# Linear attention and FFN on one core: W1 loads regrouped, the order table solved anew, warm-up matmuls of 512 columns

## The chip, the cores and the metric

The kernel runs on one core of a Trainium2 chip. The metric is the device time of one execution in microseconds (us); a kernel is quoted by the median of its fast executions, with the range. The kernel before took 301.82 us (301.79 to 301.85, 3 runs). Every later comparison has its own runs of the kernel before on the same chip, so that only numbers of one table row belong together. Three executions in the whole study took 479, 588 and 743 us, 1.6 to 2.5 times the usual time; they are called the slow executions below, and no comparison uses them.

## The reference, cut to what matters

```python
# q, k, v: (8 batches, 8 heads, 576 tokens, 64)
q_s = softmax(q, over the 64)          # per token
k_s = softmax(k, over the 576 tokens)  # per column
kv  = einsum('bhsd,bhse->bhde', k_s, v)
attn = einsum('bhsd,bhde->bhse', q_s, kv)
x = attn.transpose(0, 2, 1, 3).reshape(4608, 512)
h = x @ w_in                            # 512 x 2048
g = where(h > 0, h, exp(min(h, 0)) - 1) # ELU
return g @ w_out                        # 2048 x 512
```

Nearly all the arithmetic is the two large products: 576 matmuls of 128 x 128 by 512 columns for each of them.

## The kernel before: the parts that the argument touches

The 4608 tokens go through in nine blocks of 512. For a block, the first product runs in eight groups, each of 8 matmuls (two tiles of 128 features by four slices of 128 inputs); VectorE and ScalarE turn each group into a part of `GT` (ELU), and the second product reads `GT` as its stationary side.

Every engine works through a fixed list. The program first describes all operations, numbered as they are described; a table `ORDER` then says in which order each engine issues them. Nothing is decided at run time but the waits.

```python
ORDER = {
    "pe": (
        "30 28 32 45 43 47 50 67 54 68 69 70 77 81 85 92 114 102 89 128 136 127 135 129 137 106 130 "
        "138 108 149 151 125 148 156 133 131 155 150 139 157 152 145 172 174 158 171 173 232 238 237 "
        # ... (cut; lists for act, dve, gp and sp follow)
```

Group g of the first product, in whole or in two halves (two of the four input slices each):

```python
    def hg_mm(self, j, g, ps, key, half=None):
        # ... (cut)
            for t in range(2):
                tt = 2 * g + t
                for kc in kcs:
                    last = e.matmul(P[:, t * 512:(t + 1) * 512],
                                    self.W1[:, kc, tt * 128:(tt + 1) * 128],
                                    self.XT[:, kc, rc:rc + BLK], start=(kc == 0), stop=(kc == 3))
```

The W1 loads, the first block's order of groups, and the warm-up matmuls, which fill TensorE's idle time at the start:

```python
        for g0, g1, half in ((0, 2, 0), (0, 2, 1), (2, 5, None), (5, 8, None)):
            self.load_w1(g0, g1, half, -30, [gate, self.ident] if half == 0 else ())
        # ... (cut)
        S.spare = lambda count: lambda e: [e.matmul(
            self.PS[0][:, 0:128], self.ID[:, :], self.ID[:, :], start=True, stop=True)
            for _ in range(count)][-1]
        # ... (cut)
        for half in range(2):
            for g in range(2):
                self.hg_mm(0, g, turns[g], key, half)
        for g in range(8):
            self.hg(0, g, turns[g], key, "da"[g % 2], g > 1)
```

The softmax here doesn't subtract the row's maximum and nothing guards it: scores larger than these inputs give would overflow.

## Time and profile before

| quantity | before |
| --- | --- |
| median time | 301.82 us |
| TensorE busy | 285.5 us of a span of 300.2 |
| first product of the first block | 14.78 us |
| wait for W1's third load | 1.28 us, ending at 20.96 |
| TensorE clock at full speed from | 12.80 us |
| other holes of TensorE after 50 us that exceed 0.2 us | one, 0.34 us at 66.68 |

In the code lines of this kernel L403 is a transpose, L456 the product k x v ("kv"), L487 the attention product ("ao"), L543 the first large product, L588 the second, L653 a warm-up matmul; L572, L576 and L578 are VectorE's part of the ELU, L559 and L570 ScalarE's. Of the names, `PS` is the memory for TensorE's results, `XT` the attention result that the first product reads, `qsT` the transposed q and `MBLK` the scaled kv result that the attention product reads, and `ESB` the exponentials of the ELU. In kernels whose table is a few lines longer the same lines are shifted by the same few lines.

A table of stretches (start and end, length, then busy us and number of instructions for PE, PEld, DVE, ACT and POOL; then granted clock, DMA share, GB/s). TensorE's timeline (start, length, engine, line, operation, count).

```profile
52.00:60.00 8.00, 8.00 (x103) 6.43 (x104) 7.08 (x8) 7.70 (x9) 1.30 (x2) 1.00 1.09 317
60.00:68.00 8.00, 7.83 (x58) 5.81 (x45) 7.58 (x14) 7.03 (x8) 0.00 (x0) 1.00 1.02 272
68.00:80.00 12.00, 12.00 (x55) 9.74 (x54) 6.90 (x9) 11.74 (x14) 0.00 (x0) 1.00 0.84 229
```

**A measure used below.** Idle times tell of one hole at a time. To see where a lead is won and lost, I use a "lag": each matmul that the trace records is given the step that it takes unhindered (0.2267 us for a 512-column product, 0.0125 for one kv matmul, 0.14 for an attention product, 0.056 for a transpose, none for warm-up), these are summed in order of time, and the lag is the start time less that sum (its own step included), averaged over the matmuls that start within 1 us of the stated time. A lag that grows means that TensorE waited or ran slowly; two kernels are compared at one time by the difference. All kernels do the same work, so the lag at 290 us orders the profiled runs.

### The profile page before, as it was taken

Reading aid. Unit: us, or ns where it says so; the run is one execution under the profiler, and the core shown is the slowest. Engines: PE = TensorE matmul, PEld = TensorE weight load, DVE = VectorE, ACT = ScalarE, POOL = GpSimd, SP = SyncE. Lnnn points to the kernel's source line nnn. Section 1 sums busy time; section 2 is a strip of 40 time slices with the busy share of each in tenths; the row PEclk is TensorE's granted clock in tenths of the full one; section 3 lists DMA queues with packets and bytes.
Section 4 is the critical chain, followed back from the end, with each engine's and each line's share of the span. In section 5 each row is a group of like instructions: output and inputs, shape, how many; then the busy total and the mean of one; then the engine's idle time right before and its main releaser. Section 6 shows DMA issues by size and latency. Waiting matters only on the chain.

```text
span 300.2 us, 4404 instructions
## 1 busy us (share of the span) xinstructions
PE 285.5 (95%) x1846; PEld 234.1 (78%) x1846; DVE 188.8 (63%) x244; ACT 181.5 (60%) x211; POOL 22.1 (7%) x33
## 2 busy tenths in 40 slices
PE   0789999999999999999999999999999999999995
PEld 0658877878888888888888888888888888888883
DVE  2957954898496768766767783878355436565500
ACT  5847948989868676673966677835441623434211
POOL 0950155100000000000000000000000000000000
PEclk9999999999999999999999999999999999999999
DMA  7999996999367593569931958203221201031224
GB/s 263 387 382 391 389 359 234 309 284 265 105 212 240 126 311 70 188 143 239 295 67 41 261 149 227 59 2 70 59 58 29 61 11 35 0 90 38 49 52 105
DMA packets 35283, 49.96 MB, mean 166 GB/s; under 512 B 16320, under 2 KB 16320, under 8 KB 35264
## 3 DMA queue, kind: packets, MB, share of 16 engines
q1 hardware_dynamic: 29680, 34.09, 41.0%
q0 software_dynamic: 5504, 15.47, 15.9%
q8 instruction: 14, 0.23, 0.3%
q10 hardware_dynamic: 80, 0.13, 0.1%
q14 instruction: 5, 0.04, 0.0%
HBM read 36.70 MB, written 9.44 MB: 154 GB/s over the span
## 4 chain that ended last, share of the span: by engine, by line
PE 88%; DMA 5%; DVE 4%; POOL 1%; ACT 1%; SPq 0%; issue 0%
PE PS L588 43%; PE PS L543 40%; DMA W<-in_moe_w_in_dram 3%; PE PS L487 3%; DMA KR<-in_k_dram 2%; PE PS L456 1%; DVE GT L578 1%; POOL W L332 1%; DVE ESB L576 1%; DVE QS L380 0%; DVE ZQ L372 0%; DVE GT L572 0%; DVE MBLK L469 0%; ACT ESB L559 0%; PE PS L403 0%; SPq L315 0%
## 5 line engine op out<-in xcount | busy, mean ns | idle before, releaser
L543 PE MATMUL PS<-XT,W 128*128 128x512 f32 x576 | 140.8, 391 | 1.9 <-DMA W<-in_moe_w_in_dram 1.3
L588 PE MATMUL PS<-W,GT 128*128 128x512 f32 x576 | 141.2, 391 | 0.0
L543 PEld LDWEIGHTS PS<-XT,W 128*128 128x128 f32 x576 | 106.9, 188 | 25.1 <-DMA W<-in_moe_w_in_dram 1.7
L588 PEld LDWEIGHTS PS<-W,GT 128*128 128x128 f32 x576 | 107.1, 188 | 21.9 <-DVE GT L572 0.3
L559 ACT ACTIVATE ESB<-PS 128x1024 f32<-128x1024 f32 x72 | 73.6, 1027 | 68.9 <-PE PS L543 67.1
L576 DVE TENSOR_SCALAR ESB<-ESB 128x1024 f32<-128x1024 f32 x64 | 44.1, 691 | 73.3 <-ACT ESB L559 72.8
L578 DVE TENSOR_TENSOR GT<-ESB,PS 128x1024 fp32r<-128x1024 f32 x64 | 77.8, 1218 | 1.8
L605 ACT ACTIVATE OSB<-PS 128x512 f32<-128x512 f32 x32 | 18.6, 596 | 23.8 <-PE PS L588 23.8
L509 ACT ACTIVATE XT<-PS 128x512 fp32r<-128x512 f32 (+6 forms) x32 | 19.4, 609 | 16.5 <-PE PS L487 14.7
L372 DVE TENSOR_REDUCE ZQ<-QR 128x18 f32<-128x1152 f32 x16 | 21.5, 1346 | 5.0 <-ACT QR L352 4.9
L380 DVE TENSOR_TENSOR QS<-QR,RZQ 128x1152 f16<-128x1152 f32 x16 | 21.7, 1356 | 0.3
L352 ACT ACTIVATE QR<-QR 128x1152 f32<-128x1152 f32 x16 | 18.6, 1161 | 3.1 <-DMA QR<-in_q_dram 3.1
L356 ACT ACTIVATE KR<-KR 128x1152 bf16<-128x1152 f32 x16 | 18.5, 1160 | 0.5 <-DMA KR<-in_k_dram 0.5
L487 PE MATMUL PS<-qsT,MBLK 128*128 128x320 f32 (+5 forms) x64 | 14.2, 307 | 0.1
L431 ACT ACTIVATE qsT<-QT 128x1152 fp32r<-128x1152 f16 x12 | 14.0, 1166 | 0.3 <-DMA QT<-QS 0.3
L365 ACT ACTIVATE VB<-VR 128x1152 bf16<-128x1152 f32 (+1 forms) x12 | 13.5, 1125 | 0.8 <-DMA VR<-in_v_dram 0.8
L487 PEld LDWEIGHTS PS<-qsT,MBLK 128*128 128x128 f32 x64 | 11.4, 190 | 3.1 <-DVE MBLK L469 1.1
L572 DVE SCALAR_TENSOR_TENSOR GT<-PS,ESB 128x1024 fp32r<-128x1024 f32 x8 | 9.8, 1222 | 3.6 <-ACT ESB L570 3.6
L403 PE MATMUL PS<-ID,QS 128*128 128x128 f16 x36 | 3.2, 244 | 9.1 <-DVE QS L380 9.1
L403 PEld LDWEIGHTS PS<-ID,QS 128*128 128x128 f16 x36 | 2.5, 112 | 9.6 <-DVE QS L380 9.1
L469 DVE TENSOR_TENSOR MBLK<-PS,RZK 64x128 fp32r<-64x128 f32 x32 | 9.1, 283 | 0.8
L570 ACT ACTIVATE ESB<-ESB 128x1024 f32<-128x1024 f32 x8 | 8.4, 1056 | 0.2
(28 smaller groups left out, 58.8 us busy)
## 6 DMA issues: line engine op xcount, KB each, us to landing
out_dram<-OSB SPq DMA_DIRECT2D x63, 128.0 KB, 2.4
QR<-in_q_dram SPq DMA_DIRECT2D x12, 576.0 KB, 4.9
KR<-in_k_dram SPq DMA_DIRECT2D x12, 576.0 KB, 5.8
VR<-in_v_dram SPq DMA_DIRECT2D x12, 576.0 KB, 5.6
W<-in_moe_w_out_dram POOLq DMA_DIRECT2D x4, 1024.0 KB, 19.3
W<-in_moe_w_in_dram POOLq DMA_DIRECT2D x4, 768.0 KB, 10.3
QR<-in_q_dram POOLq DMA_DIRECT2D x4, 576.0 KB, 11.1
KR<-in_k_dram POOLq DMA_DIRECT2D x4, 576.0 KB, 6.0
```

The costliest lines, as they stand in the source:

```text
L352: S.add("act", t_act(1152, False), lambda e: e.activation(flat(q), flat(q), AF.Exp), key - 3, X=[f"qR{i}"], follow=self.table)
L356: S.add("act", t_act(1152, False), lambda e: e.activation(ek[:, :, :, :].rearrange("p h c d -> p (h c d)"), flat(k), AF.Exp), key - 2, X=[ ...
L372: S.add("dve", t_dve(1152), lambda e: e.tensor_reduce(self.ZQ[i][:, :, :].rearrange("p h c -> p (h c)"), q[:, :, :, :].rearrange("p h c d ...
L380: S.add("dve", t_dve(1152), lambda e: e.tensor_tensor(qso, q[:, :, :, :], rz, ALU.mult), key - 3, R=[f"qR{i}", f"RZQ{i}"], W=[f"QS{self.al ...
L487: last = e.matmul(P[:, y:y + n_], M[:, f, :], T[:, c0:c1, f * 64:f * 64 + 64], start=True, stop=True)
L509: S.add("act", t_act((h1 - h0) * n_, True), lambda e, dst=dst, src=src: e.activation(dst, src, AF.Copy), key, W=W, X=X)
L543: last = e.matmul(P[:, t * 512:(t + 1) * 512], self.W1[:, kc, tt * 128:(tt + 1) * 128], self.XT[:, kc, rc:rc + BLK], start=(kc == 0), stop ...
L559: S.add("act", t_act(1024, True), lambda e: e.activation(esb[:, :], P[:, :], AF.Exp), key, W=[f"E{i}"], X=banks)
L576: S.add("dve", t_dve(1024, 2), lambda e: e.tensor_scalar(esb[:, :], esb[:, :], 1.0, -1.0, ALU.min, ALU.add), key, X=[f"E{i}"])
L578: S.add("dve", t_dve(1024), lambda e: e.tensor_tensor(gt, esb[:, :], P[:, :], ALU.max), key, R=[f"E{i}"], W=gw, X=banks)
L588: last = e.matmul(dst, GT[:, jj, ts * 128:(ts + 1) * 128], self.W2[:, jj, :], start=(jj == 0), stop=(jj == 15))
L605: S.add("act", t_act(512, True), lambda e: e.activation(osb[:, :], src, AF.Copy), key, W=[f"O{i}0", f"O{i}1"], X=[f"b{bk}"])
```

## The change

W1's loads are cut so that group 2 comes with groups 0 and 1 in the two half loads, and groups 3-4 and 5-7 follow. The order table is solved anew, with W1's loads shifted. The warm-up matmuls become 512 columns wide, a quarter as many. The intent is to remove the wait for the third load.

```diff
-        "30 28 32 45 43 47 50 67 54 68 69 70 77 81 85 92 114 102 89 128 136 127 135 129 137 106 130 "
-        "138 108 149 151 125 148 156 133 131 155 150 139 157 152 145 172 174 158 171 173 232 238 237 "
+        "30 28 32 43 45 47 50 67 54 68 70 71 69 72 82 86 93 115 103 90 129 128 137 136 131 139 107 "
+        "130 138 109 151 152 150 126 134 149 132 156 157 158 140 173 146 153 159 172 174 175 233 238 "
 ... (the rest of TensorE's list, and the lists of the other four engines, cut)
-                count = int(idle / 80)
-                if count > 1 and all(d.end < free for d in self.spare_after):
-                    p = Op("pe", count * 57, self.spare(count), 0)
+                count = int(idle / 230)
+                if count > 0 and all(d.end < free for d in self.spare_after):
+                    p = Op("pe", count * 220, self.spare(count), 0)
 ... (cut: the third load's size is weighted in the list's own model, 1.15 -> 1.25)
-        for g0, g1, half in ((0, 2, 0), (0, 2, 1), (2, 5, None), (5, 8, None)):
+        for g0, g1, half in ((0, 3, 0), (0, 3, 1), (3, 5, None), (5, 8, None)):
 ... (cut)
-            self.PS[0][:, 0:128], self.ID[:, :], self.ID[:, :], start=True, stop=True)
+            self.PS[0][:, 0:512], self.ID[:, :], self.ID[:, :].unsqueeze(1).broadcast_to([128, 4, 128]),
+            start=True, stop=True)
 ... (cut)
-            for g in range(2):
+            for g in range(3):
                 self.hg_mm(0, g, turns[g], key, half)
-            self.hg(0, g, turns[g], key, "da"[g % 2], g > 1)
+            self.hg(0, g, turns[g], key, "da"[g % 2], g > 2)
```

Group 2 now is two operations, so every number above 70 rises by one.

## The prediction

> **What bounds the kernel now.** I read the page's parts 1 and 2 first, then the TensorE timeline, then the chain of waits of the first 30 us, then who waited for whom after that, and last the single records of the trace (starts, semaphore updates, DMA packets).
>
> Busy time by engine, and stretches of the run (us of busy time, instructions in brackets, granted clock, DMA share, GB/s):
> ```profile
> PE 285.5 (95%) x1846; PEld 234.1 (78%) x1846; DVE 188.8 (63%) x244; ACT 181.5 (60%) x211; POOL 22.1 (7%) x33
> ```
> ```profile
> 0.00:5.00 5.00, 0.00 (x0) 0.00 (x0) 0.72 (x6) 1.66 (x3) 0.49 (x5) 1.00 0.61 191
> ...
> 18.00:20.00 2.00, 1.68 (x8) 1.04 (x6) 0.13 (x1) 1.19 (x2) 1.09 (x2) 1.00 1.18 408
> 20.00:24.00 4.00, 3.04 (x13) 2.52 (x14) 3.01 (x3) 2.69 (x3) 0.00 (x0) 1.00 1.25 403
> 24.00:28.00 4.00, 4.00 (x20) 3.30 (x19) 2.82 (x3) 3.15 (x4) 0.00 (x0) 1.00 1.28 390
> ...
> 100.00:200.00 100.00, 100.00 (x724) 83.05 (x723) 71.28 (x91) 67.15 (x78) 0.00 (x0) 1.00 0.59 163
> ```
> The first PE number is what matters: from 24 us to 290 us TensorE is busy without a hole worth naming (39.84 of 40 us in 60 to 100, full elsewhere). So the end is set by when that unbroken stream starts; what happens before 24 us moves the end one for one, unless a new wait opens later. The chain and the PE timeline name the last hole:
> ```profile
> 8.11 3.22 POOL W L332 x5
> 11.33 9.59 DMA W<-in_moe_w_in_dram
> 20.92 0.04 issue
> 20.96 9.16 PE PS L543 x39
> ```
> ```profile
> 14.78 1.16 PE L543 MATMUL PS<-XT,W 128*128 128x512 f32 x4 [0.42 <-DVE XT L512]
> 16.05 0.74 PE L487 MATMUL PS<-qsT,MBLK 128*128 128x512 f32 x2
> 16.63 3.05 PE L543 MATMUL PS<-XT,W 128*128 128x512 f32 x12
> 20.96 9.38 PE L543 MATMUL PS<-XT,W 128*128 128x512 f32 x40 [1.28 <-DMA W<-in_moe_w_in_dram]
> ```
> TensorE finishes the 16 matmuls of groups 0 and 1 (both halves) at 19.68, and stands 1.28 us until the last part of the third W1 chunk (groups 2-4) has landed at 20.92. Only then can group 2 start. The semaphore of that transfer shows more: 15 of its 16 increments came between 18.57 and 19.63, the sixteenth at 20.92. One DMA engine is 1.3 us late, from here on in every following transfer. At 18.36 the packet list has one 16,384-byte packet of the instruction queue, 1.03 us long. Without it the chunk would have been there at about 19.65 and TensorE would hardly have stopped.
>
> **What the Trainium skill says.** "Runtime: NRT & Kernel Launch", section Instruction fetch mechanics: instruction memory is refilled in 16 KiB blocks of 256 instructions through a DMA queue of the sequencer's own. The trace agrees: that queue moved 14 packets, 0.23 MB, and when the first started, TensorE had 257 records behind it. "DMA: Bandwidth & Descriptors", section Why a DMA increments its semaphore by 16 and not by 1: only the full 16 means that all is there; agrees, as TensorE waited for the sixteenth alone. Its section Latency and other measured facts says engines 7 and 15 are usually slower than the others in traces, a rival cause; but the first ten loads (to 15 us) have all 16 increments within 0.45 us, so I take the fetch. "TensorE: Matmul & The Clock Gate", Part 1, What's actually happening: half clock until a window of about 3.4 us was busy, the window running freely. The trace: transposes and warm-up matmuls start every 0.107 us from 9.2 to 12.7 and every 0.056 us from 12.83, and the clock record changes at 12.8, 3.7 us after the first matmul.
>
> **The change, part by part.**
> (1) W1 chunks. Bytes before the end of group 4 stay 2.5 MB, so groups 3-4 land when groups 2-4 did; group 2 moves ahead, into the two half loads, which grow from 0.5 to 0.75 MB each. From the landings (first W1 load from about 12.35, each 256 KB 0.67 us): first half done at 12.35+2x1.0 = 14.35 instead of 13.67, needed at 14.78; second half at 16.4 instead of 15.0, needed at 17.58. Both have room (0.4 and 1.2 us). Groups 3-4 land at about 19.6, or 20.9 if a fetch falls into them again.
> (2) TensorE order there. The new list has group 0 and 1 as before, then group 2's two halves, then group 3. Group 2 is 8 matmuls at 0.227 to 0.231 us (steps of the trace) = 1.83 us, so group 3 is wanted at 19.52+1.83 = 21.35, after even the late landing of 20.9. The 1.28 us wait goes, and with it the slow first step after a wait (0.335 against 0.23 us: 0.1). **Gain 1.4 us.** Groups 5-7 still land at 24.83; they are wanted at 21.35+16x0.227 = 24.98: just in time.
> (3) Warm-up. 18 matmuls of 128 columns become a handful of 512. Time filled is about the same (four 0.107 us steps = one cold 512-column step), and they fill gaps; but 13 fewer matmuls are 26 fewer TensorE instructions, which moves the first instruction fetch later by about as much, to 19 us or later. I count nothing for it, since (2) tolerates it.
> (4) New order at the start. VectorE now reduces the second q before it scales the first. From the DVE rows (1.27 us between such starts) the first transposes move from 9.12 to about 10.4 us. Walking the lists with the measured durations: scaling of the second q ends near 11.9 as before, ScalarE's second k exponential starts near 12.2 (11.5 before) and its half of the v copy ends near 13.95 (13.2), the second kv at 14.0 (13.88); the first XT copies end at about 15.1 (14.67) as the qsT copy now goes before one of them; but the second MBLK is ready at 15.8 (16.0), so TensorE no longer pauses between group 0 and the second ao: that ao at about 16.1 (16.05), group 1 at 16.6 (16.63). **Net 0, give or take 0.3.** The price is in the clock: TensorE is now busy from 10.4, not 9.1. If full speed comes one window (3.4 us) later, at 16.2, the first ao and some of group 0 run at 0.43 instead of 0.23 us a matmul: about 3 x 0.2 = 0.6 us lost on the path. I give this half a chance: **0.3 us**.
> (5) Order after 24 us. TensorE has no wait there to win back; loads of q, k, W2 and v change places but their sum stays, and DMA is full until about 44 us.
> Sum: 301.8 - 1.4 + 0.3 = 300.7 us.
>
> **The rivals.**
> First, the gain is given back later. DMA runs at about 390 GB/s until 44 us whatever TensorE does, so a TensorE that is 1.4 us early meets the same landings. The fourth v lands at 44.76, GpSimd converts it by 45.97, TensorE takes it at 47.70: 1.7 us of room, 1.4 used. The third W2 slice lands at 39.01 and is used at 40.85: 1.8 us of room. These rows speak against a new wait, but narrowly; if the last W2 slice, now behind a k load (some 1.5 us later than 41.56), or v came late, a third to all of the gain would go: 301 to 301.8.
> Second, the clock. The late-clock case of (4) as a whole, with a longer second cold window, makes it 301.0 to 301.5. For it: the work now starts later. Against: the warm-up matmuls are meant to prevent it, and W1's landing no longer has to be hidden.
> Third, ScalarE or VectorE becomes the bound in block 0. Per pair of groups they need 2x1.03+1.06 = 3.1 us and 0.69+1.22+1.22 = 3.1 us against TensorE's 16x0.227 = 3.63; they keep up, so I give this little. It would cap the gain at about 1 us.
> Fourth, more than 1.4: new order closing small losses (8 matmuls take 2.04 instead of 1.81 us now and then between 38 and 105 us). Perhaps 0.5 us: 300.0.
>
> **Range and chances.** The middle is 300.7. Best case (clock on time, small losses closed) 299.9; gain lost to a later wait and the clock together 301.9. A 2% change is 6 us; all idle time of TensorE between its first matmul and its last is about 2 us and nothing in the change shortens a matmul, so faster by 2% is nearly impossible, and slower by 2% would take a wait of 7 us that nothing here suggests.
>
> **What would show it right or wrong.** The new profile's PE timeline should have no wait on W1 near 20 us, with group 2 starting near 19.5 and group 5 near 25.0; the sixteenth increment of the groups 3-4 load may still be late. The first transposes should start near 10.4; the step of the first 512-column matmuls after 14.8 tells the clock (0.23 or 0.43). Between 32 and 60 us TensorE should show no new wait on W2, v or the kv results. The prediction is wrong if the second half of W1 arrives after 17.6 us, if groups 5-7 are waited for near 25 us, if TensorE stands for the fourth v near 46 us, or if the first XT comes much later than 15.1.

## More of the kernel before

What follows a group before its result can be used (variant "d": ScalarE exp, then two VectorE operations):

```python
        S.add("act", t_act(1024, True), lambda e: e.activation(esb[:, :], P[:, :], AF.Exp), ...)
            # ... (cut)
            S.add("dve", t_dve(1024, 2), lambda e: e.tensor_scalar(
                esb[:, :], esb[:, :], 1.0, -1.0, ALU.min, ALU.add), key, X=[f"E{i}"])
            S.add("dve", t_dve(1024), lambda e: e.tensor_tensor(
                gt, esb[:, :], P[:, :], ALU.max), key, R=[f"E{i}"], W=gw, X=banks)
```

```profile
52.53 5.60 PE L543 MATMUL PS<-XT,W 128*128 128x512 f32 x24
57.97 1.52 PE L588 MATMUL PS<-W,GT 128*128 128x512 f32 x6
```

The reader should see three things. TensorE is full from 52 to 60 us. But so, nearly, are VectorE (7.08 of 8) and ScalarE (7.70 of 8): the second block's ELU and the attention of later batches meet here. And before TensorE asks for the first ELU result of block 1 (L588 at 57.97), it has 24 products in a row: the last 16 of them come after group 0 is complete.

## The result, and the profile after

The changed kernel took 302.35 us (301.65 to 303.31, 6 runs), the kernel before 301.83 us (301.77 to 302.95, 6 runs) on that chip. The ratio is 1.0016, with an interval of 0.9991 to 1.004. Here and below a ratio is the mean time of one kernel's fast runs over that of the other's of the same rounds, so it is not quite the ratio of the quoted medians. The predicted gain of 1.1 us is not there, and the median lies above the predicted range. The profiled execution took 303.15 us, one of the longer two of the six.

The start of TensorE's work in the changed kernel, from the timeline (to be held against the prediction's third fence):

```profile
10.14 1.14 PE L403 MATMUL PS<-ID,QS 128*128 128x128 f16 x9 [6.36 <-DVE QS L380]
13.18 1.20 PE L487 MATMUL PS<-qsT,MBLK 128*128 128x512 f32 x2
15.71 1.20 PE L543 MATMUL PS<-XT,W 128*128 128x512 f32 x4
16.74 0.70 PE L487 MATMUL PS<-qsT,MBLK 128*128 128x512 f32 x2
17.28 13.95 PE L543 MATMUL PS<-XT,W 128*128 128x512 f32 x60
```

The wait for W1 is gone: 60 products in a row from 17.28 us. The attention product at 13.18 takes 1.20 us for two matmuls, against 0.70 at 16.74: the clock rose only at 15.48 us (before: 12.80), and the first product began at 15.71 (before: 14.78). The stretches, as above:

```profile
20.00:24.00 4.00, 4.00 (x19) 3.34 (x18) 3.38 (x4) 3.50 (x4) 0.48 (x1) 1.00 1.26 399
52.00:60.00 8.00, 7.55 (x100) 5.46 (x99) 7.73 (x9) 7.38 (x8) 1.15 (x1) 1.00 1.02 259
68.00:80.00 12.00, 11.28 (x48) 8.41 (x47) 8.04 (x9) 10.51 (x12) 0.00 (x0) 1.00 0.39 124
```

From 20 to 24 us TensorE is now full (before: 3.04 of 4). But two stretches that were full have holes: 7.55 of 8 and 11.28 of 12. The timeline names the waits (in brackets: idle time before the group and what ended it):

```profile
50.64 4.70 PE L543 MATMUL PS<-XT,W 128*128 128x512 f32 x20
55.72 1.21 PE L588 MATMUL PS<-W,GT 128*128 128x512 f32 x4 [0.38 <-DVE GT L578]
72.24 0.62 PE L487 MATMUL PS<-qsT,MBLK 128*128 128x384 f32 x2 [0.44 <-ACT qsT L431]
76.27 1.20 PE L588 MATMUL PS<-W,GT 128*128 128x512 f32 x4 [0.19 <-DVE GT L572]
```

The bracket's idle time counts from the modelled end of the last matmul. From start to start, less the usual step, the losses are 0.55 us at 55.72, 0.24 at 57.00, 0.26 at 69.24, 0.60 at 72.24 and 0.35 at 76.27: 2.0 us together, where the kernel before has 0.34 in the same stretch. The timeline of ScalarE and VectorE shows why TensorE stands at 55.72:

```profile
52.65 1.94 ACT L559 ACTIVATE ESB<-PS 128x1024 f32<-128x1024 f32 x2 [0.16 <-PE PS L543]
53.72 0.69 DVE L576 TENSOR_SCALAR ESB<-ESB 128x1024 f32<-128x1024 f32 x1
54.45 1.22 DVE L578 TENSOR_TENSOR GT<-ESB,PS 128x1024 fp32r<-128x1024 f32 x1
55.72 1.23 DVE L572 SCALAR_TENSOR_TENSOR GT<-PS,ESB 128x1024 fp32r<-128x1024 f32 x1
```

Group 0 of block 1 is complete near 52.5 us. ScalarE starts on it at 52.65, and TensorE starts on the result at 55.72: the ELU chain is 3.07 us long (one exponential, then 0.69 and 1.22 us on VectorE, with the hand-overs). Of the 20 products at 50.64, eight complete group 0; twelve remain, 12 x 0.2267 = 2.72 us. So the new list asks for the result too early. The list shows it: "172 174 175 233 238" is group 0 in two halves, then half of group 1 (4 products) and group 2 (8), then the second product. The old list has "171 173 232 238 237": group 0 in two halves, then groups 2 and 3 (16 products, 3.63 us), then the second product. In the kernel before the chain is as long, but it is hidden behind 3.63 us of work. There group 0 is complete at 54.34 us (eight steps after 52.53):

```profile
54.55 1.03 ACT L559 ACTIVATE ESB<-PS 128x1024 f32<-128x1024 f32 x1 [0.27 <-PE PS L543]
55.61 0.69 DVE L576 TENSOR_SCALAR ESB<-ESB 128x1024 f32<-128x1024 f32 x1
56.34 1.22 DVE L578 TENSOR_TENSOR GT<-ESB,PS 128x1024 fp32r<-128x1024 f32 x1
```

The result is there at 57.56 us, 3.01 us after ScalarE began, and TensorE asks for it at 57.97, 0.4 us later.

The hole at 72.24 has another origin: the transpose of a q by DMA had 15 increments of its semaphore by 69.47 and the sixteenth at 71.00 us; ScalarE waited for it. A packet of the instruction queue of 16,384 bytes ran from 68.70 for 1.11 us. At 76.27 VectorE had waited for an output store that landed late, because the store's staging memory is that of a `GT` part:

```profile
71.02 1.17 ACT L431 ACTIVATE qsT<-QT 128x1152 fp32r<-128x1152 f16 x1 [1.10 <-DMA QT<-QS]
74.99 1.23 DVE L572 SCALAR_TENSOR_TENSOR GT<-PS,ESB 128x1024 fp32r<-128x1024 f32 x1 [3.46 <-DMA out_dram<-OSBX]
```

The lag gives the balance of this run. The changed kernel leads by 14.80 - 13.86 = 0.94 us at 24 us and by 0.98 at 52. From 52 to 68 us its lag grows by 1.41 us, that of before by 0.87. From 68 to 80 it grows by 1.76 against 0.30. It ends 1.05 us behind (17.98 and 16.93 at 290 us).

### The profile page after: what moved, and what is told of

Read it like the earlier page. It is cut to its first block, busy times and chain, and to the rows that moved or that the text cites. A ratio compares the mean times of both kernels' runs of the same rounds, so it can differ in the third digit from the quotient of the medians.

```text
span 301.4 us, 4384 instructions
## 1 busy us (share of the span) xinstructions
PE 288.3 (96%) x1835; PEld 233.8 (78%) x1835; DVE 189.4 (63%) x244; ACT 182.1 (60%) x211; POOL 21.8 (7%) x33
## 3 DMA queue, kind: packets, MB, share of 16 engines
q0 software_dynamic: 5504, 15.47, 16.0%
## 4 chain that ended last, share of the span: by engine, by line
PE 88%; DVE 5%; DMA 4%; ACT 2%; SPq 1%; issue 0%; DVEq 0%
PE PS L588 42%; PE PS L543 39%; PE PS L487 3%; DMA out_dram<-OSBX 3%; PE PS L456 2%; DMA QR<-in_q_dram 1%; DVE ZQ L372 1%; DVE GT L572 1%; PE PS L403 1%; DVE QS L380 1%; ACT ESB L559 1%; PE PS L653 0%; DVE ESB L576 0%; DVE GT L578 0%; DVE MBLK L469 0%; ACT QR L352 0%
## 5 line engine op out<-in xcount | busy, mean ns | idle before, releaser
L588 PE MATMUL PS<-W,GT 128*128 128x512 f32 x576 | 141.2, 392 | 0.6 <-DVE GT L578 0.4
L588 PEld LDWEIGHTS PS<-W,GT 128*128 128x128 f32 x576 | 106.8, 188 | 22.8 <-DVE GT L578 0.8
```

What stands on the lines that cost most here:

```text
L588: last = e.matmul(dst, GT[:, jj, ts * 128:(ts + 1) * 128], self.W2[:, jj, :], start=(jj == 0), stop=(jj == 15))
```

## The experiments

Eighteen experiments ran; e9, e10, e11, e13, e14 and e17 run a kernel again. In the quoted expectations theories carry letters; I take them up here by what they say. The first question was which of the three parts (W1 chunks, order table, warm-up) does what.

### The three parts alone, and the change without its warm-up

**Chunks only (e1)**: the new W1 loads on the kernel before. Its order table is kept; where the old list had group 2 as one operation, both halves stand one after the other.

```diff
-        for g0, g1, half in ((0, 2, 0), (0, 2, 1), (2, 5, None), (5, 8, None)):
+        for g0, g1, half in ((0, 3, 0), (0, 3, 1), (3, 5, None), (5, 8, None)):
```

> The W1 chunks of the change (groups 0-2 in halves, 3-4, 5-7) in the order of the kernel before (its one entry for group 2 becomes the two halves in the same place), old warm-up of 128 columns. Theory A (the chunks gain about 1.3 us and the new order gives it back): about 300.4 us, 1.2 to 1.6 below the kernel before, no TensorE wait on W1 near 20 us, group 2 starting near 19.6 us, and the lead still there at 100 us. Rival B (a TensorE that is early always runs into the same later landings, in whatever order): no better than 301.5, with new TensorE waits between 40 and 80 us.

**Warm-up only (e2)**: the kernel before with 512-column warm-up matmuls, 5 in place of 18.

```diff
-            self.PS[0][:, 0:128], self.ID[:, :], self.ID[:, :], start=True, stop=True)
+            self.PS[0][:, 0:512], self.ID[:, :], self.ID[:, :].unsqueeze(1).broadcast_to([128, 4, 128]),
+            start=True, stop=True)
```

> The kernel before with only the warm-up changed to a quarter as many matmuls of 512 columns (18 become 5, so 26 fewer TensorE instructions). Theory A (the instruction fetch at 18.4 us is what delays the sixteenth DMA engine, and it is triggered by the instruction count): the fetch moves some 2 to 3 us later, the third W1 chunk lands near 19.6 instead of 20.9, the TensorE wait of 1.28 us falls to below 0.3 and the time by about 1 us, to 300.8. Rival B (one DMA engine is slow for another reason, or the fetch goes by time): the chunk still lands at about 20.9, and the time stays at 301.8.

**Order only (e3)**: the new table on old chunks and old warm-up.

```diff
-        "30 28 32 45 43 47 50 67 54 68 69 70 77 81 85 92 114 102 89 128 136 127 135 129 137 106 130 "
+ ... (the new lists of all five engines; the two halves of group 2, which old chunks have as one operation, merged)
```

> The new order table on the old W1 chunks with the old warm-up. Theory A (the order is what costs): slower than the kernel before by 1 to 2 us, 303 to 304, with the same TensorE stalls between 54 and 78 us as the changed kernel, about 1.5 us in sum beyond those of the kernel before, and first transposes near 10.1 us. Rival B (the order is neutral, the stalls come of TensorE being early): 301.8, stalls gone.

**The change with the old warm-up (e4)**: the changed kernel, but 128-column warm-up matmuls (21 of them).

```diff
-            self.PS[0][:, 0:512], self.ID[:, :], self.ID[:, :].unsqueeze(1).broadcast_to([128, 4, 128]),
-            start=True, stop=True)
+            self.PS[0][:, 0:128], self.ID[:, :], self.ID[:, :], start=True, stop=True)
```

> The changed kernel with the old warm-up of 128 columns (the rule then puts 12 before the first transposes, 3 and 6 later). If the wider warm-up is not what costs, the time stays at that of the changed kernel within 0.4 us (302.0 to 302.8) and it spreads as widely from run to run (more than 1 us) since the clock still rises one window late. If the warm-up is what costs, it comes down to about 301.

Measured (the kernel before: 301.88 us, 301.38 to 302.54, 11 runs):

| kernel | us, median (range) | ratio to before (interval) |
| --- | --- | --- |
| e1 chunks only | 301.04 (300.68 to 301.12) | 0.9966 (0.9953 to 0.9978) |
| e2 warm-up only | 303.19 (301.69 to 304.07) | 1.0031 (1.0009 to 1.0053) |
| e3 order only | 302.75 (302.45 to 303.64) | 1.0032 (1.0017 to 1.0047) |
| e4 change, old warm-up | 301.70 (301.13 to 302.22) | 0.999 (0.9975 to 1.0004) |

Only the chunks gain, 0.84 us by the medians, less than the 1.2 to 1.6 that was expected. Each of the other two parts alone loses about 0.9 to 1.3 us. e4 lies between the two outcomes that were named for it. In e1 TensorE does not wait for W1:

```profile
15.06 1.17 PE L546 MATMUL PS<-XT,W 128*128 128x512 f32 x4 [0.57 <-DVE XT L515]
16.75 7.59 PE L546 MATMUL PS<-XT,W 128*128 128x512 f32 x32
```

In e3 the wait is there as before, now 0.93 us by the bracket, and the new holes are there too: 0.55 us at 56.66 and 0.24 at 57.94. So these two holes come with the order table and need neither the new chunks nor the wide warm-up:

```profile
20.99 3.24 PE L546 MATMUL PS<-XT,W 128*128 128x512 f32 x13 [0.93 <-DMA W<-in_moe_w_in_dram]
```

e2 missed what was expected of it. In its profiled run, its fastest, the first instruction fetch had moved from 18.36 to 22.31 us, the last increment of W1's third load came at 19.86 and the wait was gone, as foreseen. But the clock rose at 15.05 us (before: 12.80), and the first product started at 15.87. The other five runs were up to 2.4 us longer, which this profile doesn't show.

### The clock at the start, and the number of instructions

**e5** and **e6** issue 16 wide warm-up matmuls early, as soon as the identity matrix is there, on the changed kernel and on e1. **e8** keeps the changed kernel's wide matmuls and adds 14 of two columns, so that the count of warm-up matmuls is 21 as in e4. **e7** was to carry the new order at the start and the old one behind it.

```diff
 e5, e6:
-                count = int(idle / 80)
-                if count > 1 and all(d.end < free for d in self.spare_after):
+                if not out or not any(x.eng == "pe" for x in out):
+                    p = Op("pe", 16 * 220, self.spare(16), 0)
 e7: new lists up to the first block's end, old lists from there (SyncE's old throughout), old warm-up
 e8:
+            for w in [2] * 14 + [512] * count
```

> The changed kernel, its 7 warm-up matmuls replaced by 16 of 512 columns that run from 1.9 us on, ahead of the first transposes. Theory C (the spread of the changed kernel and part of its loss come of the TensorE clock rising one free-running window, 3.4 to 6.8 us, after its work starts, and the removed W1 wait no longer hides this): the clock is up between 5.3 and 8.7 us, all matmuls after 14.8 us step at 0.23 us from the first, the time falls by 0.6 to 1.0 us to some 301.5, and the spread of runs shrinks from 1.7 us to below 0.8. Rival D (the clock's phase does not matter): time and spread as the changed kernel's, 302.3 and over 1.2 us.

> The first experiment (new W1 chunks, old order), its 18 warm-up matmuls of 128 columns replaced by 16 of 512 from 1.9 us on. Theory C: group 0 starts near 14.5 instead of 15.06 us and the second ao near 15.8 instead of 16.2; about 0.4 us faster than that experiment, 300.6 us. Rival D: 301.0 as that experiment.

> The changed kernel with the old warm-up, with the new order only up to the start of block 1 (about 50 us) and the order of the kernel before from there, DMA queue of SyncE in the old order throughout. Theory A2 (the new order loses its time after 50 us: the TensorE waits on VectorE's gate results at 55 to 58 us, 0.8 us in sum): 0.7 to 0.9 us faster than the changed kernel with old warm-up (301.7), so 300.8 to 301.0, and no TensorE hole over 0.5 us after 50 us. Rival (the new order loses its time in the first 20 us): 301.7, as that one.

> The changed kernel with 14 matmuls of 2 columns added ahead of its first warm-up group, so that TensorE has as many instructions as with the old warm-up (21 warm-up matmuls), but the wide ones stay. Theory E (the wide warm-up costs because 28 fewer instructions move TensorE's instruction fetches under other transfers, such as the transpose at 66 to 71 us): time as with the old warm-up, 301.7. Rival (the wide warm-up costs by its own time or by the clock): as the changed kernel, 302.35.

This chip was restless (the kernel before: 302.06 us, 301.17 to 303.99). The fast runs of e5 span 300.62 to 302.57 us, ratio 0.9987 (0.9956 to 1.0019), and its profile fell in a slow execution: nothing follows. e7's fast runs took 303.12 us or more, ratio 1.0055 (1.0021 to 1.0089); it joins lists that were not solved together, its profile too was of a slow execution, and it says nothing about the cause. e8 had 301.86 us (300.86 to 303.19), ratio 0.9989 (0.996 to 1.0018).

e6 gave 301.84 us (300.70 to 302.78), ratio 0.9976 (0.9947 to 1.0005), where 300.6 was hoped for, and its profile (302.78 us) shows what a lost clock costs. The stretches are those of the clock's own windows of 3.41 us; the first number after the comma is TensorE's busy time, the third from the end the granted clock:

```profile
7.00:10.40 3.40, 1.54 (x13) 0.70 (x11) 3.30 (x5) 2.03 (x3) 1.82 (x3) 1.00 1.05 398
10.40:13.80 3.40, 2.63 (x47) 1.95 (x47) 2.87 (x6) 3.40 (x6) 3.40 (x7) 0.50 1.15 391
13.80:17.20 3.40, 2.91 (x42) 2.30 (x42) 1.94 (x5) 0.96 (x2) 3.40 (x5) 0.50 1.17 377
17.20:20.60 3.40, 3.40 (x9) 2.63 (x9) 0.69 (x1) 0.60 (x1) 2.37 (x4) 0.50 1.22 407
```

The early matmuls raised the clock at 7.00 us. They were over at 7.9, and after a window with 1.54 us of work the clock fell at 10.41. The next two windows, 77% and 86% busy, did not raise it; only the one that was full did, at 20.65. A share of 86% is not too little in every case, though: in e14 below, the window before the clock's rise at 13.02 us was 86% busy too (2.92 of 3.41 us). Until then a 512-column product took 0.427 us. At 24 us this run's lag is 15.57, against 13.32 in e1: 2.25 us lost.

**e9** repeats e2, **e10** the changed kernel and **e11** repeats e8 on another chip. **e12** is e1 with seven wide warm-up matmuls at the very start, which wait for the first exponential, so that they join the transposes without a gap, and with the old warm-up behind them.

```diff
 e12, against e1:
+                if not any(x.eng == "pe" for x in out):
+                    p = Op("pe", 7 * 427, self.spare7, 0)
+                    p.deps = {self.ops[22]: "raw", self.spare_after[0]: "raw"}
+                    out.append(p)
```

> One more look at the second experiment (the kernel before with the 5 wide warm-up matmuls), whose profiled run was its fastest (301.7) while most of its runs were at 303.2. Theory C (clock): in a slow run the clock is up later than 15.1 us, at 18 to 20 us, and TensorE's 512-column matmuls step at 0.43 us until then, 1 to 2 us lost before 22 us. Theory E (fetch): the clock is as before, and TensorE stops for over 0.5 us somewhere between 60 and 120 us, behind a transposing transfer or a store whose one engine was held by an instruction fetch. If the run is again a fast one (under 302), nothing follows.

> The changed kernel itself, unaltered, on the chip of the other runs of this call, to compare with and for a second profile. Both theories: 302.0 to 302.7 with a spread of over 1 us. If the holes at 69 to 76 us of its first profile are of the moved fetch and are the rule, they are here again; if they were of that one run, they are gone and this run is under 302.

> The same 14 matmuls of 2 columns added to the changed kernel as in the eighth experiment, which fell on a restless chip. Theory E (the number of TensorE instructions places the fetches): 0.4 to 0.8 us faster than the changed kernel of this same call. Rival (only width or clock): the same within 0.2 us.

> New W1 chunks, old order, old warm-up, and 7 more matmuls of 512 columns that wait for the first exponential, so TensorE is busy from 6.0 us without a break up to its first transposes. Theory C: the clock is up between 9.4 and 12.9 us in each run instead of between 12.4 and 15.8, so the second transposes and the first ao run at full speed; 0.1 to 0.5 us faster than the first experiment's gain of 0.9, that is about 1.0 to 1.3 below the kernel before, spread under 0.4 us. Rival D: the first experiment's gain of 0.9 us, no more; if the 14 added instructions move a fetch badly, less.

The kernel before took 302.15 us here (301.63 to 302.72, 11 runs). e9's one run took 303.84 us; the state of a single run is unknown. Its first fetch came at 19.34 us, not at 22.31 as in e2, and the wait for W1 was back:

```profile
21.83 2.34 PE L543 MATMUL PS<-XT,W 128*128 128x512 f32 x9 [1.17 <-DMA W<-in_moe_w_in_dram]
```

One and the same program thus fetches up to 3 us earlier or later, and with the fetch the last part of the load comes at 19.86 or 21.79 us. e10, the changed kernel, had fast runs from 301.39 to 302.44 us, ratio 0.9995 (0.998 to 1.001); its profile was of the 479 us execution, so the holes at 69 to 76 us could not be looked for again. e11 had 301.89 us (301.05 to 303.03), ratio 0.9989 (0.9968 to 1.001). The difference of 0.06% is within the noise: whether the number of warm-up instructions costs time is not settled.

e12 is the best version: **300.30 us (300.12 to 300.56), ratio 0.9939 (0.9926 to 0.9952)**, 1.85 us below the kernel before by the medians, where 1.0 to 1.3 was expected. TensorE is busy without a gap from 5.90 us until the clock rises at 11.29, and the second transposes and the attention product already run at full speed:

```profile
5.90 3.17 PE L665 MATMUL PS<-ID 128*128 128x512 f16 x7 [5.90 <-ACT QR L360]
12.04 0.67 PE L411 MATMUL PS<-ID,QS 128*128 128x128 f16 x9
12.66 0.73 PE L495 MATMUL PS<-qsT,MBLK 128*128 128x512 f32 x2
14.96 1.16 PE L551 MATMUL PS<-XT,W 128*128 128x512 f32 x4 [0.79 <-DMA W<-in_moe_w_in_dram]
```

Now the first half load of W1, larger than before the change, is what the first product waits for. The spread of the fast runs is 0.44 us, as in e1 and less than in e1's repeat e13 below (1.59). A clock that always rises in time would explain a small spread and the larger gain, but e12 never ran beside e1.

### Where the order table loses

Two calls asked whether the stretch near 55 us is what costs. **e13** and **e14** repeat e1 and e4 as bases, **e15** is e14 with the old order in that stretch alone, and **e16** has the old order until about 43 us and the new one from there (new chunks, old warm-up, SyncE's list new throughout).

```diff
 e15, against e14 (numbers of the new list):
-  pe:  159 172 174 175 233 238 237 239 192 243 249 245 244 251 250
+  pe:  175 159 172 174 233 239 238 237 244 192 243 245 251 250 249
-  dve: 148 155 182 183 184 177 178 232
+  dve: 155 148 182 183 184 232 177 178
-  act: 147 166 154 169 205 176 230 231 188 234 180
+  act: 154 147 180 166 230 169 231 176 205 188 234
```

> New W1 chunks alone, again, as the base of this call. All theories: about 0.8 us below the kernel before, no TensorE hole between 55 and 59 us.

> The changed kernel with the 128-column warm-up, again, as the other base. All theories: 0.5 to 0.8 us above the chunks alone, with TensorE holes of about 0.55 and 0.25 us near 55.5 and 56.8 us.

> The same changed kernel with 128-column warm-up, but in one stretch (about 47 to 62 us) the order of before on TensorE, VectorE and ScalarE. Theory F (the new order loses its lead because TensorE is given the first W2 products of block 1 before VectorE has made their gate results): both holes near 55 to 58 us go, and the time falls by 0.5 to 0.8 us, to about 0.1 to 0.2 us above the chunks alone. Theory G (the new order loses by its start before 20 us or by many small losses later): the holes may go, but the time stays within 0.2 us of the changed kernel with 128-column warm-up.

> The order of before until about 43 us, the new order from there on, new W1 chunks, 128-column warm-up. Theory F: the first products of group 0 start as early as with the chunks alone, near 15.1 us, but the holes near 55 to 58 us are there and it ends 0.6 to 0.8 us above the chunks alone. Theory G: near the chunks alone, within 0.3 us.

Measured (the kernel before: 301.91 us, 301.08 to 304.02): e13 301.31 us (300.74 to 302.33), ratio 0.9978; e14 301.62 (301.20 to 302.60), 0.9987; e15 302.48 (302.24 to 304.06), 1.0028; e16 303.60 (302.45 to 305.50), 1.0059. The intervals are about 0.003 wide to either side. Neither theory had this. In e15 both holes of 55 to 58 us went, but a larger one opened where the old stretch begins (and one of 0.58 us at 63.16):

```profile
50.36 1.20 PE L543 MATMUL PS<-XT,W 128*128 128x512 f32 x4 [0.91 <-DVE XT L512]
```

In the old list a group's products stand between the attention products and the operation that needs their copies; my cut had left them on the other side of it. e16 has a hole of 2.18 us at 58.11, again at L588 and again for VectorE's result, then six products in a row at 0.427 us: after the stop the clock fell as well, its record has it at half speed from 59.15 to 62.57 us.

**e17** repeats e14's kernel, and **e18** moves e15's cut three places ahead in TensorE's list, and VectorE's behind the results of group 3:

```diff
 e18, against e17:
-  pe:  173 146 153 159 172 174 175 233 238 237 239 192 243 249 245 244 251 250
+  pe:  153 146 173 175 159 172 174 233 239 238 237 244 192 243 245 251 250 249
-  dve: 148 155 182 183 184 177 178 232 206 235 236 193 194 207 195 196 197 242 208
+  dve: 155 148 182 183 184 232 177 178 206 235 236 193 207 194 242 195 208 196 197
 (act as in e15)
```

> The changed kernel with the 128-column warm-up, as the base of this call: holes of about 0.55 and 0.25 us near 55 and 56 us, about 0.2 us below the kernel before.

> As e15, with the cut of the TensorE list moved three places ahead, so that the first products of group 1 stand between the attention products and the second ones again (in e15 TensorE waited 0.91 us there for XT, because the filling stayed behind the cut), and the cut of VectorE's list moved behind the results of group 3. Theory F: no hole over 0.2 us between 46 and 62 us, and the time falls by 0.6 to 1.0 us against e17. Theory G: the holes go and the time stays within 0.2 us of e17. If a new hole of the same size opens in or just behind the stretch, neither is told apart.

e17 had 301.21 us (300.90 to 301.76), ratio 0.9971; e18 302.99 us (302.05 to 304.49), 1.0032; the kernel before 301.90. Again the stretch waits elsewhere:

```profile
48.68 0.79 PE L487 MATMUL PS<-qsT,MBLK 128*128 128x256 f32 x4 [0.93 <-DVE MBLK L469]
58.23 1.67 PE L588 MATMUL PS<-W,GT 128*128 128x512 f32 x6 [0.47 <-DVE GT L578]
```

With the filling moved ahead, nothing covers the path from the kv product to the attention product (0.93 us). And L588 waits again although 16 products now stand before it. ScalarE began on group 0 at 54.22 us, 0.3 after its last product, but VectorE's first operation then took 1.40 us instead of 0.69, while GpSimd copied a v:

```profile
55.22 1.15 POOL L368 CAST VB<-VR 128x1152 bf16<-128x1152 f32 x1 [4.23 <-DMA VR<-in_v_dram]
55.51 1.40 DVE L576 TENSOR_SCALAR ESB<-ESB 128x1024 f32<-128x1024 f32 x1
```

It is not a matter of one profile. In all twenty such a VectorE operation started during such a copy four times (e7, e10, e16 and e18), and took 1.00 to 1.42 us; all others took at most 0.72. In e16 it was the same operation on group 0 (1.42 us at 55.38). The 0.71 us more is longer than e18's hole at 58.23 (0.63 from start to start), so without the collision this hole would not have been there (an estimate). A list that is moved thus meets work on an engine that nobody moved.

The condition stated before e18 holds: a new hole of the same size opened, and by removal the two theories are not told apart. None of the four transplanted stretches (e7, e15, e16, e18) was faster than either list whole.

What can be read without a transplant is the lag, from every profile in a fast run that was not a transplant (e9's single run is counted in). Growth of the lag in us:

| profile (us of that run) | table | lag at 24 us | 52 to 60 | 60 to 68 | 68 to 80 | lag at 290 us |
| --- | --- | --- | --- | --- | --- | --- |
| before (302.05) | old | 14.80 | 0.16 | 0.71 | 0.30 | 16.93 |
| e1 (300.68) | old | 13.32 | 0.15 | 0.70 | 0.39 | 15.58 |
| e13 (301.41) | old | 13.78 | 0.10 | 0.76 | 0.66 | 16.31 |
| e12 (300.56) | old | 12.99 | 0.16 | 0.65 | 0.73 | 15.47 |
| e2 (301.69) | old | 14.28 | 0.15 | 0.70 | 0.42 | 16.56 |
| e9 (303.84) | old | 15.64 | 0.16 | 0.68 | 1.15 | 18.72 |
| e6 (302.78) | old | 15.57 | 0.16 | 0.67 | 0.32 | 17.68 |
| after (303.15) | new | 13.86 | 1.20 | 0.21 | 1.76 | 17.98 |
| e3 (302.66) | new | 14.80 | 1.21 | 0.11 | 0.41 | 17.48 |
| e4 (301.64) | new | 13.57 | 1.15 | 0.38 | 0.39 | 16.45 |
| e14 (301.71) | new | 12.97 | 1.12 | 0.41 | 1.05 | 16.51 |
| e17 (301.28) | new | 13.16 | 1.13 | 0.24 | 0.40 | 16.09 |
| e8 (301.66) | new | 13.46 | 1.11 | 0.56 | 0.39 | 16.48 |
| e11 (301.87) | new | 13.95 | 1.19 | 0.19 | 0.39 | 16.70 |

From 52 to 60 us the old table loses 0.10 to 0.16 us in seven profiles and the new one 1.11 to 1.21 in seven. Some of it is back by 68 us, since the old table has a wait near 66 us that the new one has only in part: from 52 to 68 us the old loses 0.81 to 0.87 and the new 1.32 to 1.67. So the new table's net loss there is some 0.5 to 0.8 us, in every run, and it fits what the times say of the table on the new chunks: e4 less e1 is 0.66 us and e14 less e13 0.31 (the second is within the noise). e3, the table alone, shows it most plainly: it is level with the kernel before at 24 us (14.80 each) and 0.55 us behind at 290, of which 0.45 arise from 52 to 68 us and 0.11 from 68 to 80. At 24 us the new table is no worse (e4, e14 and e17: 12.97 to 13.57; e1 and e13: 13.32 and 13.78).

The loss at 68 to 80 us is of another kind: it is 0.3 to 0.4 us in most profiles and up to 1.76 in some, with both tables. In the two largest cases (after, e9) an instruction fetch started at 68.70 and 69.53 us, in no other profile of this table between 68 and 70, and in both the sixteenth increment of the q transpose came 1.5 us after the fifteenth (71.00 and 71.71 us). But e14 lost 1.05 us with its fetches at 63.07 and 84.48: there VectorE waited for a store whose sixteenth increment came at 73.44 us, the others by 72.36. A fetch beside the q transpose thus fits two cases, and is not the only cause of a late increment.

## Why the prediction was wrong, point by point

**(1) and (2), the W1 chunks: right in mechanism, too large in size.** No profile with the new chunks shows a wait between groups 2 and 3; an increment as late as 20.63 us (e1) does no harm, as the step said. The term was 1.4 us. Alone it was worth 0.84 us by the medians of e1 (0.0034 of 302 = 1.0 by the ratio), 0.6 in e13 (where the interval still holds 0). Taking the wait away lays the start open, which the wait had hidden: whatever the clock or the copies cost before 16 us now moves the end, and e1 and e13 differ by 0.46 us at 24 us with the same program.

**(3), the warm-up: "I count nothing for it" was wrong.** The step looked only at the filled time and the fetch. Fewer and wider matmuls alone cost 1.3 us in e2 (0.3 to 1.6 by the interval). In the changed kernel the cost is smaller and not cleanly measured: its ratio was 1.0016 and 0.9995, with the old warm-up 0.999, 0.9987 and 0.9971, so about 0.1 to 0.3%, an estimate across chips. The fetch did not stay where the step put it either: it moved by 3 us between two runs of one program. Nor is the count of 257 TensorE records at which the prediction saw it start a fixed one: it was 231 in e9, 239 in the changed kernel and 246 in e1.

**(4), the start: right.** The first transposes began at 10.14 us (10.4 was said), the clock rose late, at 15.48, and the case that had half a chance and 0.3 us in the sum came in full: the first product came at 15.71 instead of 15.2, the second attention product at 16.74 instead of 16.1. That is 0.5 to 0.6 us against 0.3. Even so the profiled run led by 0.94 us at 24 us, near the 1.1 that the sum gave.

**(5), "TensorE has no wait there to win back": this is the step that failed.** It asked what a new table could win after 24 us and never what it could lose. The new table puts 12 products where 16 stood between group 0 of block 1 and the use of its result, 2.72 us of work before a chain of 3.07 us. Every profile of that table shows the hole, and no profile of the old table does. The net cost is 0.5 to 0.8 us. In the profiled run another 1.46 us (1.76 - 0.30) went at 68 to 80 us, where part of the runs of both tables lose time.

**The rivals.** The first one, "the gain is given back later", was the right outcome with the wrong carrier: it watched the landings of v and W2, and none of them was waited for. The third, VectorE or ScalarE as the bound, was weighed in block 0 and by throughput; what bound was the latency of one pass through both engines, in block 1. The second, the clock, came true but was the smaller part. The fourth, a gain of more than 1.4 us, did not come.

**Summed up:** the chunks bring 0.6 to 1.0 us, the table takes 0.3 to 0.9 and the warm-up about as much (estimates, partly across chips); nothing is left. What stays open: how much of the warm-up's cost is the clock and how much the place of the fetches; and, by removal, the price of the hole at 55 us, since no mended table was made that keeps the rest.

## What to carry to other kernels

When a change brings a new order, count the work that each list puts between a result's last input and its first use, and hold it against the latency of the chain between; a list of numbers in a diff can be read that way before anything runs. It is not enough alone: in e18 the work was there and TensorE waited all the same, because another engine's copy lengthened the chain. A gain at the start is worth only what no later wait takes back, so every list behind it belongs in the prediction, as a cost too. If two parts of a change lose and one gains, as here, take the one: the new chunks with the old table, and warm-up matmuls that reach without a gap from early on to the first real work, were 1.85 us faster than the kernel before.

## What the Trainium skill lacked or had wrong

- "Runtime: NRT & Kernel Launch", Instruction fetch mechanics, calls the cost of crossing a block "mostly hidden". It says nothing of loads that are in flight beside the fetch: with a fetch at 18.36 us one of sixteen increments of W1's third load came at 20.92, the others by 19.63, and TensorE waited 1.28 us. In two runs of one program, with the fetch at 22.31 and at 19.34 us, that last increment came at 19.86 and at 21.79. The fetch is not the only cause of a late increment, as e14 shows above.
- "TensorE: Matmul & The Clock Gate", Part 1, What's actually happening, asks for a busy window and gives no share that counts as busy. In e6 windows of 77% and 86% by the profile did not raise the clock, and a full one did; in e14 a window of 86% did raise it. So the share that the profile shows, with its modelled ends of matmuls, does not decide it. A window of 45% (1.54 of 3.40 us) let it fall.
- The same section: the time from the start of continuous work to full speed was 2.9 us in e14, 3.7 in the kernel before, 5.3 in the changed one, 5.4 in e12 and 6.0 in e2, where the page names a budget of about 3.4 us and a variation of 500 ns.
- No page has whole executions that take 1.6 to 2.5 times as long: 479, 588 and 743 us among runs of 300 to 306 us, on two chips; the clock record of the first shows 0.555 from 13.34 to 433.55 us.
